# Tiles of token sums turned once per attention unit, with later loads and statistics and with stores on SyncE's queue

## The chip, the cores and the metric

One core of a Trainium2 chip runs the whole kernel. The metric is the device time of one execution in microseconds (us); smaller is better.

## The reference, cut to what matters

```python
# attention, for each of 8 batches and 8 heads, 576 tokens, head size 64
q_s = softmax(q, axis=-1)              # over the head's channels
k_s = softmax(k, axis=2)               # over the tokens
attn = q_s @ (k_s^T @ v)               # heads side by side: x [8, 576, 512]
# first mixer (weights moe_*)
h = relu(x^T @ w_tok1) @ w_tok2        # mixes tokens, 576 -> 256 -> 576
u = x + h^T
y = u + relu(u @ w_ch1) @ w_ch2        # mixes channels, 512 -> 1536 -> 512
# second mixer (weights moe2_*)
yn = (y - mean(y)) / sqrt(var(y) + 1e-6) * g_ln
out = y + relu(yn @ w2_ch1) @ w2_ch2   # 512 -> 2048 -> 512
```

## The kernel before

Each product is made of three passes on parts of float32 (PASSES), so the kernel is bound to many matmuls on TensorE (PE). The 4608 tokens are cut into nine blocks of 512: block j below 8 holds the first 512 tokens of batch j, and block 8 (B in the code) holds the 64 last tokens of every batch.

**The first mixer's channel part** is the class Phase1. A block takes 12 steps f. A step makes one tile of hidden rows (L1, line 748, PSUM tile ph), its ReLU and rest on ScalarE (ACT, line 170) and VectorE (DVE, line 171), and adds a hidden tile made two steps earlier to four accumulators (L2, line 765, tile acc). ph has two buffers, so that L1 of step f needs DVE's h of step f - 2. The order of the blocks is: two steps of block 0, block 1, the rest of block 0, blocks 2 to 7, block 8. The hidden weights of block 0 and 1 come in from HBM in the same stretch.

**Work beside the matmuls** is put into the program by a counter of ticks. `later(n, fn)` runs fn at the n-th next tick, and every step has four ticks: one within L1, one behind the ReLU, one within L2, one at the end. A tick is a place in program order, not a time: each engine goes through its own instructions in order and waits for what it needs. SyncE (SP) holds only DMA issues, so it runs ahead until one of them has to wait; what stands behind that one waits too. The same holds for DMAs that are issued on ACT, where arithmetic stands behind them.

**Attention** is the class Unit: one unit is a batch and two heads. The first eight run before the steps. Then four units run beside each block from the end of block 1 until the end of block 6, ten ticks apart (GAP), in a chain k_max (DVE, line 472), k_top (PE transpose, line 493, DVE, line 495: tile kmd), k_sub (PE transpose of kmd, line 506, tile pb; POOL, line 514, and then the loads of the next unit's k and q, on SP), q_exp, q_norm, q_split, kv (PE, line 555, and then the load of the next unit's v, on SP), tok1, hidden, tok2. q_turn turns the unit's softmax in 32x32 pieces on DVE, q_move stores that tile (zq) to HBM from ACT's queue, and q_load brings it back by rows from SP's queue, which completes the transposition for q_T.

**The sums y** of a block are completed by Phase1.finish, which runs in the second step of the next block: DVE adds u to the accumulators (line 787, tile yT, one buffer), POOL adds the rest of u for each of four chunks of 128 tokens (line 793), and yT goes to HBM as it is. For the second mixer the sums are needed by tokens too. For each chunk c, YAT + YGAP * c ticks behind finish, y_turn turns the pieces on DVE (line 678, tile z), one tick later y_move stores z from ACT's queue (line 685), three ticks after that y_load loads it by rows on SP's queue (line 692, tile yn), and three ticks after that y_stat takes mean and variance on DVE (lines 696 and 697). z and yn take turns in the two buffers of one tag. Block 8 has another way, y_store: four transposes on PE into PSUM (line 702), one copy on ACT (line 707), a store from ACT's queue (line 711), and y_stat directly on that copy.

**Root** makes 1/sqrt of the variances of blocks 0 to 6 (`Root(0, B - 1)`, 37 ticks into block 7) and brings them to HBM; a second Root does this for blocks 8 and 7 in the second mixer.

**The second mixer's weights** are prepared beside blocks 2 to 8. Sums goes through jobs, two of them per step: `first`, `bits` and `add` on DVE and ACT, `out` (ACT and POOL, lines 885 and 886, tile so), `store` (line 963, on ACT's queue), `load` (line 915, on ACT's queue). Rows (in blocks 7 and 8, one run per step) loads rows on SP (line 978, tile xr), decodes them on ACT and DVE (lines 873, 877, 880), splits them (lines 885 and 886) and stores from POOL's queue. In block 8, the second mixer's first inputs are loaded (load_x, line 1126; load_mr, line 1143), normalized by POOL (hat, line 1150), scaled by ACT (gain) and split and subtracted (lines 1159, 1160 on DVE, 1165 on POOL).

**The second mixer** follows with products (line 1263) and their sums (line 1301), with 48 steps and no attention.

Of the kernel before, what the change touches and what calls it, by code (L numbers as in the profile page):

```python
# [8 lines left out]
F32 = mybir.dt.float32  # L9
# [7 lines left out]
P = 128  # L17
# [7 lines left out]
def kernel(  # L25
# [23 lines left out]
    nc = tc.nc  # L49
    B, H, S, D = q.shape  # L50
    DM = H * D
# [18 lines left out]
    NB = NT // BLK  # L70
    CT = BLK // P
    LAG = 2
    YAT, YGAP = 3, 5
    HT = 3 * P
    SB = 2 * HT
    NS = NT // SB
# [6 lines left out]
    main = ctx.enter_context(tc.tile_pool(name="main", bufs=1))  # L83
# [7 lines left out]
    y_dram = dram.tile([NB, CT, 4, P, P], F32, name="y_dram")  # L91
    q_dram = dram.tile([2, P, W], F32, name="q_dram")
    yT_dram = dram.tile([NB, P, KD, BLK], F32, name="yT_dram")
# [81 lines left out]
    extra, bufs = [], []  # L175
# [164 lines left out]
    def later(n, fn):  # L340
        ticks.setdefault(now[0] + n, []).append(fn)
# [92 lines left out]
    class Unit:  # L434
# [7 lines left out]
        def start(self, at):  # L442
            steps = (
                self.k_max, self.k_top, self.q_max, self.q_sub, self.k_sub, self.q_exp,
                self.q_norm, self.k_exp, self.q_split, self.kv, self.tok1,
                lambda: self.q_T(0), self.hidden, lambda: self.q_T(1),
                lambda: self.tok2(0), lambda: self.tok2(1), self.q_turn, self.q_move, self.q_load,
            )
            if self.early:
                when = (0, 1, 1, 1, 3, 3, 4, 5, 7, 8, 10, 10, 11, 12, 14, 15)  # L450
            else:
                when = (0, 2, 1, 2, 4, 4, 5, 6, 8, 8, 10, 13, 12, 99, 15, 16, 7, 8, 10)
            if 0 < self.n < 3:
                k = (12, 8)[self.n - 1]
                when, steps = when[k:], steps[k:]
            for n, fn in zip(when, steps):
                if n < 99:
                    later(at + n, fn)
# [163 lines left out]
            )  # L622

        def q_move(self):
            nc.scalar.dma_start(out=q_dram[self.n % 2], in_=self.zq)

        def q_load(self):
            self.qz = self.zq
# [45 lines left out]
    yT_t, yn_t, yz = {}, {}, {}  # L674
# [7 lines left out]
        yz[j, c] = z  # L682

    def y_move(j, c):
        nc.scalar.dma_start(out=y_dram[j, c].rearrange("q t w -> (q t w)").rearrange("(p n) -> p n", p=P), in_=yz.pop((j, c)))

    def y_rows(j, c):
        return y_dram[j, c].rearrange("q t w -> t q w")
# [1 line left out]
    def y_load(j, c):  # L690
        yn_t[j, c] = main.tile([P, DM], F32, tag="t", bufs=2, name="yn")
        nc.sync.dma_start(out=yn_t[j, c].rearrange("p (q w) -> p q w", q=4), in_=y_rows(j, c))

    def y_stat(j, c, yn):
        st = main.tile([P, 6], F32, tag="st6", bufs=2, name="st6")
        nc.vector.bn_stats(out=st, in_=yn)
        nc.vector.bn_aggr(out=mr[:, pos[j], :, c], in_=st)

    def y_store(j, c):
        pt = psum("py")  # L700
        for kk in range(KD):
            nc.tensor.transpose(
                out=pt[:, kk * P:(kk + 1) * P], in_=yT_t[j][:, kk, c * P:(c + 1) * P],
                identity=ident,
            )
        yn = yn_t[j][:, c * DM:(c + 1) * DM]
        nc.scalar.activation(
            out=yn.rearrange("p (q k e) -> p k q e", q=4, k=KD), in_=pt[:, 0:DM].rearrange("p (k q e) -> p k q e", q=4, k=KD),
            func=AF.Copy,
        )  # L710
        nc.scalar.dma_start(out=y_rows(j, c), in_=yn.rearrange("p (q w) -> p q w", q=4))
        y_stat(j, c, yn)
# [7 lines left out]
    class Phase1:  # L720
# [51 lines left out]
        def finish(self, dds=range(KD)):  # L772
            if self.f1 < NF1:
                t = [main.tile([P, 512], F32, tag="t", bufs=2, name="part") for _ in range(2)]
                x = att.tile([P, 2, 512], F32, tag="qx", name="part")
                for dd, o in enumerate((t[0], t[1], x[:, 0], x[:, 1])):
                    nc.scalar.activation(out=o, in_=self.acc[dd], func=AF.Copy)
                for dd in range(2):
                    nc.sync.dma_start(out=part_dram[:, dd], in_=t[dd])
                nc.sync.dma_start(out=part_dram[:, 2:4], in_=x)  # L780
                return
            if not dds[0]:
                yT_t[self.j] = main.tile([P, KD, BLK], F32, tag="y", bufs=1, name="yT")
            yT, u = yT_t[self.j], u_t[self.j]
            for dd in dds:
                x = self.part[dd // 2][:, dd % 2] if self.f0 else u[:, 0, dd].bitcast(F32)
                nc.vector.tensor_tensor(out=yT[:, dd], in0=self.acc[dd], in1=x, op=ALU.add)
            if dds[-1] < KD - 1:
                return

            def add(c):
                x = slice(c * P, (c + 1) * P)
                nc.gpsimd.tensor_tensor(
                    out=yT[:, :, x], in0=yT[:, :, x], in1=u[:, 1, :, x].bitcast(F32), op=ALU.add
                )

            if self.j == B:
                return add
            later(26, lambda: nc.sync.dma_start(out=yT_dram[self.j], in_=yT))
            for c in range(CT):  # L800
                if self.f0 == 0:
                    later(2 * c if self.j > 1 else 0, lambda c=c: add(c))
                n = YAT + YGAP * c
                later(n, lambda c=c: y_turn(self.j, c))
                later(n + 1, lambda c=c: y_move(self.j, c))
                later(n + 4, lambda c=c: y_load(self.j, c))
                later(n + 7, lambda c=c: y_stat(self.j, c, yn_t.pop((self.j, c))))


    class Root:  # L810
# [81 lines left out]
    class Sums:  # L892


        def __init__(self):
            self.st = None
            self.jobs = [lambda: self.load(0), nop]
            for n in range(2 * NP):
                self.jobs += [
                    self.first, self.bits, self.add, lambda n=n: self.out(n, 0), self.store,  # L900
                    lambda n=n: self.out(n, 1),
                    lambda n=n: (self.store(), self.load(n + 1)), nop,
                ]

        def run(self):
# [54 lines left out]
                self.done = (wd_dram[g, :, kk], o[:, :, 0:3])  # L960

        def store(self):
            nc.scalar.dma_start(out=self.done[0], in_=self.done[1].bitcast(F32))

    class Rows:

# [37 lines left out]
    with tc.manual_schedule():  # L1004
# [162 lines left out]
        for o, f in steps:  # L1167
# [6 lines left out]
            if f == 0:  # L1174
                if 1 < o.j < B - 1:
                    for hp in range(NHP):
                        Unit((o.j + 1) * NHP + hp).start(OFF + hp * GAP)
                elif o.j == B - 1:
                    att.release()
                    w2pool = tc.alloc_tile_pool(name="w2pool", bufs=1, reuse_waits="tile")  # L1180
                    mix_rows.append(Rows(w2pool))
                    later(20, load_ends)
                    Root(0, B - 1).start(37)
            if o.j <= 1:
                loads.until(len(tok) + 4 * (f // 2) + 2)
            if o.j == B:
# [195 lines left out]
            at((0, 0, 0, 1, 3)[n - 3], (4, 5, 6, 0, 1)[n - 3], lambda n=n: load_w2(n))  # L1382
        at(1, 3, more_acc)
        at(2, 6, other_h)
        root = Root(B - 1, NB)
        at(5, 0, root.root)
        at(5, 2, root.rstd)
        at(5, 4, root.scatter)
# [88 lines left out]
```

## Time and profile before

| what | value |
|---|---|
| median of 3 runs | 1611.84 us (1611.59 to 1618.25) |
| profiled execution, its own time | 1613.86 us |
| its span, first to last instruction | 1612.1 us |
| PE busy | 1563.9 us (97%) |
| DVE, ACT, POOL busy | 892.8 us (55%), 482.8 us (30%), 511.8 us (32%) |
| mean granted clock of PE | 0.993 |
| one half step of blocks 7 and 8, 12 matmuls | 2.72 us |
| steps of blocks 2 to 6 with attention, read from block to block | 92 to 93 us for 12 steps |

Busy time of PE is near the whole span, so what counts is where PE stands still, what it waits for there, and how fast it runs (the granted clock, 1.00 for 2.4 GHz and 0.50 for 1.2 GHz). The busy times of the other engines say little, since most of their idle time is waiting for PE.

### The profile page before, as it was taken

The numbers are of one execution on the slowest core, as the hardware profiler recorded it, in microseconds if no ns is written. First come the engines' busy times: TensorE is split into PE (matmuls) and PEld (weight loads), VectorE is DVE, ScalarE is ACT, GpSimd is POOL, SyncE is SP. The second block draws the span as 40 slices with busy tenths as digits, with TensorE's granted clock in tenths as the row PEclk, the third lists the DMA queues.
The fourth block names the chain that finished last, engine by engine and source line by source line (L and its number), as shares of the span: only waits on it lengthen the run. The fifth ranks groups of instructions, "written<-read, shape, count | busy, mean of one in ns | idle before, by whom it ended". The sixth has DMA issues, their size and how long they took to land.

```text
span 1612.1 us, 21480 instructions
## 1 busy us (share of the span) xinstructions
PE 1563.9 (97%) x7993; PEld 1369.3 (85%) x7993; DVE 892.8 (55%) x1625; ACT 482.8 (30%) x976; POOL 511.8 (32%) x424
## 2 busy tenths in 40 slices
PE   5999999999999999999989999999999999999998
PEld 4988888888887878887868989999898999989897
DVE  7775657677675857757774445335335335325333
ACT  5664323333233333323231222222222222213111
POOL 5744613343342535333561402210310310311000
PEclk9999999999999999999989999999999999999999
DMA  7562534545463654548777566346355445444351
GB/s 184 162 206 72 134 122 130 165 138 172 120 179 115 175 144 137 157 155 316 231 271 274 192 144 217 130 148 206 121 174 181 148 157 176 152 150 162 115 168 39
DMA packets 212221, 263.46 MB, mean 163 GB/s; under 512 B 98958, under 2 KB 168646, under 8 KB 203670
## 3 DMA queue, kind: packets, MB, share of 16 engines
q1 hardware_dynamic: 184534, 204.22, 40.9%
q10 hardware_dynamic: 22528, 40.80, 7.7%
q0 software_dynamic: 5056, 17.08, 2.9%
q8 instruction: 63, 1.03, 0.3%
q14 instruction: 40, 0.33, 0.1%
HBM read 199.62 MB, written 62.43 MB: 163 GB/s over the span
## 4 chain that ended last, share of the span: by engine, by line
PE 82%; DMA 7%; DVE 4%; POOL 2%; ACT 2%; issue 2%; SPq 0%; ACTq 0%; DVEq 0%; POOLq 0%
PE pp L1263 22%; PE acc L1301 17%; PE ph L748 14%; PE acc L765 12%; PE acca L1301 8%; PE pu L649 4%; DMA yn<-y_dram 3%; PE pg L585 2%; PE pk L555 1%; DMA wc_dram<-so 1%; PE ph L634 1%; DMA st<-in_moe_w_ch 1%; DMA zq<-q_dram 1%; DMA stages<-in_moe_w_tok 1%; DMA y_dram<-z 1%
## 5 line engine op out<-in xcount | busy, mean ns | idle before, releaser
L1263 PE MATMUL pp<-xc,wr 128*128 128x384 f32 x2016 | 393.3, 338 | 0.0
L1263 PEld LDWEIGHTS pp<-xc,wr 128*128 128x128 f32 x2016 | 359.6, 188 | 19.3 <-DVE sc L1276 0.4
L748 PE MATMUL ph<-u,w 128*128 128x512 f32 x1296 | 325.7, 398 | 9.8 <-DVE h L171 9.8
L765 PE MATMUL acc<-h,w 128*128 128x512 f32 x1296 | 319.7, 393 | 0.0
L748 PEld LDWEIGHTS ph<-u,w 128*128 128x128 f32 x1296 | 241.1, 191 | 60.3 <-DVE h L171 11.5
L765 PEld LDWEIGHTS acc<-h,w 128*128 128x128 f32 x1296 | 238.6, 188 | 47.5
L1301 PE MATMUL acc<-w,hh 128*128 128x512 f32 x648 | 180.6, 393 | 0.0
L1301 PEld LDWEIGHTS acc<-w,hh 128*128 128x128 f32 x648 | 121.3, 188 | 26.6
L1301 PE MATMUL acc<-w,h 128*128 128x512 f32 x501 | 143.6, 394 | 0.0
L1150 POOL TENSOR_TENSOR xs<-xs 128x768 f32<-128x768 f32 x48 | 89.8, 1901 | 153.1 <-DMA xs<-mr_dram 127.9
L170 ACT ACTIVATE hh<-sc 128x384 fp32r<-128x384 f32 x96 | 50.5, 526 | 238.7 <-DVE sc L1276 236.2
L171 DVE SCALAR_TENSOR_TENSOR h<-ph,h 128x512 fp32r<-128x512 f32 x108 | 73.7, 684 | 82.3 <-ACT h L170 81.9
L1276 DVE TENSOR_TENSOR sc<-su,pp 128x384 f32<-128x384 f32 x144 | 79.6, 553 | 66.2 <-PE pp L1263 65.6
L1276 DVE TENSOR_TENSOR su<-su,pp 128x384 f32<-128x384 f32 x96 | 53.1, 553 | 111.6 <-PE pp L1263 111.2
L1301 PE MATMUL acca<-w,hh 128*128 128x512 f32 x432 | 114.2, 391 | 0.0
L170 ACT ACTIVATE h<-ph 128x512 fp32r<-128x512 f32 x108 | 64.1, 595 | 139.1 <-PE ph L748 130.6
L1301 PEld LDWEIGHTS acc<-w,h 128*128 128x128 f32 x501 | 92.5, 188 | 12.2
L171 DVE SCALAR_TENSOR_TENSOR hh<-sc,hh 128x384 fp32r<-128x384 f32 x96 | 63.6, 662 | 63.3 <-ACT hh L170 63.3
L1301 PEld LDWEIGHTS acca<-w,hh 128*128 128x128 f32 x432 | 80.5, 188 | 14.0
L886 POOL TENSOR_TENSOR so<-st,so 128x512 fp32r<-128x512 f32 (+2 forms) x48 | 40.2, 853 | 116.9 <-ACT so L885 102.3
L1321 POOL DMA_DIRECT2D out<-sd x5 | 2.9, 582 | 224.8 <-DVE sd L1314 224.8
L649 PE MATMUL pu<-w,hs 128*128 128x288 f32 x384 | 62.2, 298 | 0.0
(191 smaller groups left out, 1951.8 us busy)
## 6 DMA issues: line engine op xcount, KB each, us to landing
wr<-wc_dram SPq DMA_DIRECT2D x48, 1024.0 KB, 4.8
wr<-wd_dram SPq DMA_DIRECT2D x48, 768.0 KB, 4.4
yT_dram<-yT SPq DMA_DIRECT2D x9, 1024.0 KB, 9.1
yb<-y_dram SPq DMA_DIRECT2D x36, 256.0 KB, 6.2
y_dram<-z ACTq DMA_DIRECT2D x32, 256.0 KB, 2.6
yn<-y_dram SPq DMA_DIRECT2D x32, 256.0 KB, 3.6
st<-in_moe_w_ch ACTq DMA_DIRECT2D x16, 512.0 KB, 5.5
wc_dram<-so ACTq DMA_DIRECT2D x16, 512.0 KB, 3.1
```

Of the source, the lines that this page charges most:

```text
L170: nc.scalar.activation(out=hi, in_=x, func=AF.Relu)
L171: nc.vector.scalar_tensor_tensor(out=lo, in0=x, scalar=0.0, in1=hi.bitcast(F32), op0=ALU.max, op1=ALU.subtract)
L555: nc.tensor.matmul(out=pk[:, 0:2 * D + 2], lhsT=self.kt[:, c], rhs=vts[self.n % 2 if self.early else 0][:, c, :], start=(c == 0), stop=(c ...
L585: nc.tensor.matmul(out=pg[:, 0:T], lhsT=self.qn[:, x, c], rhs=w1[:, y, c, :], start=(n == 0), stop=(n == len(terms) - 1),)
L649: nc.tensor.matmul(out=pu[:, 0:HN], lhsT=l, rhs=r, start=(n == 0), stop=(n == len(terms) - 1))
L748: nc.tensor.matmul(out=ps, lhsT=w[:, x, kk, fo:fo + P], rhs=u[:, y, kk], start=(n == 0), stop=(n == 3 * KD - 1),)
L765: nc.tensor.matmul(out=self.acc[dd], lhsT=w[:, x, f % 2, dd * P:(dd + 1) * P], rhs=h[:, y], start=(f == self.f0 and n == 0), stop=(f == se ...
L886: nc.gpsimd.tensor_tensor(out=o[:, 1], in0=x, in1=o[:, 0].bitcast(F32), op=ALU.subtract)
L1150: nc.gpsimd.tensor_tensor(out=y, in0=y, in1=m, op=(ALU.subtract, ALU.mult)[op])
L1263: nc.tensor.matmul(out=bank[(BANK[i] + q) % 2][:, 0:HT], lhsT=r[:, kk, x], rhs=xc[i][:, y, kk], start=(n == 0 and not add), stop=(n == 5), ...
L1276: nc.vector.tensor_tensor(out=o, in0=x, in1=y, op=ALU.add)
L1301: nc.tensor.matmul(out=acc[c], lhsT=h[:, x, m * P:(m + 1) * P], rhs=wb2[p][:, f, y], start=(p == 0 and n == 0), stop=(p == NP - 1 and n == 5),
```

## The change

- YAT goes from 3 to 5 and YGAP from 5 to 10: the four chunks of a block are turned ten ticks apart, the distance of the attention units. y_load comes 5 ticks behind y_turn instead of 4, and y_stat 14 ticks behind it instead of 7.
- y_move, q_move and the stores of Sums are issued on SP's queue instead of ACT's. q_turn and q_move stand ahead of q_split and kv among the instructions of their ticks. A store of Sums is issued at once behind its `out`; the number of jobs stays eight.
- POOL's additions for blocks 2 to 6 come 3, 5, 7 and 8 ticks behind finish instead of 0, 2, 4 and 6. yT goes to HBM 18 ticks behind finish instead of 26.
- Block 7 (B - 1) uses y_store, 5, 7, 9 and 11 ticks behind finish, in place of y_turn, y_move, y_load and y_stat.
- Root for blocks 0 to 5 starts 24 ticks into block 7; the second Root takes blocks 6, 8 and 7.

```diff
-    YAT, YGAP = 3, 5
+    YAT, YGAP = 5, 10
...
-                self.q_norm, self.k_exp, self.q_split, self.kv, self.tok1,
+                self.q_norm, self.k_exp, *(() if self.early else (self.q_turn, self.q_move)), self.q_split, self.kv, self.tok1,
                 lambda: self.q_T(0), self.hidden, lambda: self.q_T(1),
-                lambda: self.tok2(0), lambda: self.tok2(1), self.q_turn, self.q_move, self.q_load,
+                lambda: self.tok2(0), lambda: self.tok2(1), self.q_load,
...
-                when = (0, 2, 1, 2, 4, 4, 5, 6, 8, 8, 10, 13, 12, 99, 15, 16, 7, 8, 10)
+                when = (0, 2, 1, 2, 4, 4, 5, 6, 7, 8, 8, 8, 10, 13, 12, 99, 15, 16, 10)
...
-            nc.scalar.dma_start(out=q_dram[self.n % 2], in_=self.zq)
+            nc.sync.dma_start(out=q_dram[self.n % 2], in_=self.zq)
...
-        nc.scalar.dma_start(out=y_dram[j, c].rearrange("q t w -> (q t w)").rearrange("(p n) -> p n", p=P), in_=yz.pop((j, c)))
+        nc.sync.dma_start(out=y_dram[j, c].rearrange("q t w -> (q t w)").rearrange("(p n) -> p n", p=P), in_=yz.pop((j, c)))
...
-        yn = yn_t[j][:, c * DM:(c + 1) * DM]
+        yn = yn_t[B][:, c * DM:(c + 1) * DM] if j == B else main.tile([P, DM], F32, tag="t", bufs=2, name="yn")
...
-            later(26, lambda: nc.sync.dma_start(out=yT_dram[self.j], in_=yT))
+            later(18, lambda: nc.sync.dma_start(out=yT_dram[self.j], in_=yT))
...
-                    later(2 * c if self.j > 1 else 0, lambda c=c: add(c))
+                    later((3, 5, 7, 8)[c] if 1 < self.j < B - 1 else 2 * c * (self.j > 1), lambda c=c: add(c))
+                if self.j == B - 1:
+                    later(5 + 2 * c, lambda c=c: y_store(self.j, c))
+                    continue
...
-                later(n + 4, lambda c=c: y_load(self.j, c))
-                later(n + 7, lambda c=c: y_stat(self.j, c, yn_t.pop((self.j, c))))
+                later(n + 5, lambda c=c: y_load(self.j, c))
+                later(n + 14, lambda c=c: y_stat(self.j, c, yn_t.pop((self.j, c))))
...
-                    self.first, self.bits, self.add, lambda n=n: self.out(n, 0), self.store,
-                    lambda n=n: self.out(n, 1),
-                    lambda n=n: (self.store(), self.load(n + 1)), nop,
+                    self.first, self.bits, self.add, lambda n=n: (self.out(n, 0), self.store()), nop,
+                    lambda n=n: (self.out(n, 1), self.store()),
+                    lambda n=n: self.load(n + 1), nop,
...
-            nc.scalar.dma_start(out=self.done[0], in_=self.done[1].bitcast(F32))
+            nc.sync.dma_start(out=self.done[0], in_=self.done[1].bitcast(F32))
...
-                    Root(0, B - 1).start(37)
+                    Root(0, B - 2).start(24)
...
-        root = Root(B - 1, NB)
+        root = Root(B - 2, NB)
```

## Rows read from the trace of the kernel before

**Rows 1.** Windows by stretch: us, busy (x instructions) by engine, clock, DMA share, GB/s

```profile
85.00:805.00 720.00, 705.92 (x3600) 596.98 (x3599) 485.21 (x898) 250.36 (x511) 290.72 (x254) 1.00 0.53 159
805.00:860.00 55.00, 47.22 (x199) 39.10 (x198) 37.89 (x38) 15.93 (x28) 26.99 (x19) 0.91 0.64 240
860.00:1612.00 752.00, 745.91 (x3715) 671.14 (x3713) 307.06 (x512) 165.38 (x316) 137.67 (x99) 1.00 0.49 161
```

**Rows 2.** Waits of PE from 85 to 805 us: total us, times, longest

```profile
PE pb L506 <- DVE kmd L495: 8.5, 9, 2.3
PE ph L748 <- DVE h L171: 2.0, 2, 1.3
```

**Rows 3.** Timeline from 427 to 581 us: start, duration, operation [idle before <- releaser]

```profile
428.09 0.32 PE L506 MATMUL pb<-ident,kmd 128*128 128x128 f32 x1 [0.19 <-DVE kmd L495]
...
570.37 1.31 SPq L692 DMA_DIRECT2D yn<-y_dram  x1
...
578.53 0.69 DVE L696 BATCH_NORM_STATS2 st<-yn 128x6 f32<-128x512 f32 x1 [6.42 <-DMA yn<-y_dram]
...
580.75 0.32 PE L506 MATMUL pb<-ident,kmd 128*128 128x128 f32 x1 [2.33 <-DVE kmd L495]
```

**Rows 4.** Waits of DVE from 85 to 705 us

```profile
DVE st L696 <- DMA yn<-y_dram: 28.2, 5, 6.4
```

**Rows 5.** Windows of the three stretches at the lower clock behind 85 us

```profile
581.29:584.70 3.41, 3.41 (x13) 2.92 (x12) 2.86 (x3) 0.72 (x2) 1.71 (x1) 0.50 0.03 8
809.98:816.80 6.82, 5.08 (x12) 4.02 (x13) 6.72 (x9) 2.16 (x4) 3.72 (x3) 0.50 0.42 151
833.88:837.28 3.40, 3.40 (x9) 2.64 (x8) 2.17 (x2) 0.00 (x0) 2.44 (x2) 0.50 1.02 425
```

**Rows 6.** Waits of PE from 805 to 860 us

```profile
PE ph L748 <- DVE h L171: 7.7, 2, 5.1
```

**Rows 7.** Timelines of DVE and POOL from 800 to 834 us

```profile
802.51 0.69 DVE L696 BATCH_NORM_STATS2 st<-yn 128x6 f32<-128x512 f32 x1 [6.84 <-DMA yn<-y_dram]
...
805.67 4.43 DVE L880 SCALAR_TENSOR_TENSOR xr<-xr 128x512 uint32<-128x512 uint32 x1
810.03 1.07 DVE L678 STREAM_TRANSPOSE z<-yT 128x512 f32<-128x512 f32 x1
...
825.24 7.43 DVE L1160 TENSOR_TENSOR xc<-xs,xc 128x768 fp32r<-128x768 f32 x1
...
805.98 3.57 POOL L1150 TENSOR_TENSOR xs<-xs 128x768 f32<-128x768 f32 x2
...
822.82 7.25 POOL L1150 TENSOR_TENSOR xs<-xs 128x768 f32<-128x768 f32 x4
```

**Rows 8.** DMA issues of the page: count, KB each, median us from issue to landing

```profile
y_dram<-z ACTq DMA_DIRECT2D x32, 256.0 KB, 2.6
yn<-y_dram SPq DMA_DIRECT2D x32, 256.0 KB, 3.6
...
y_dram<-xs ACTq DMA_DIRECT2D x4, 256.0 KB, 8.0
```

**Rows 9.** Lines of PE, then its timeline around the first such group

```profile
L702 PE MATMUL py<-ident,yT 128*128 128x128 f32 x16 | 2.4, 272 | 0.0
...
861.58 0.60 PE L702 MATMUL py<-ident,yT 128*128 128x128 f32 x4
...
861.93 1.29 PE L1263 MATMUL pp<-xc,wr 128*128 128x384 f32 x6
```

**Rows 10.** Waits of SP from 85 to 705 us, then timelines of SP and DVE

```profile
SPq L353 <- POOL kt L514: 139.8, 23, 10.1
...
449.45 1.25 SPq L353 DMA_DIRECT2D rawk<-in_k  x2
...
460.19 1.28 DVE L472 TENSOR_REDUCE kmx<-rawk 128x128 f32<-128x640 f32 x1
```

**Rows 11.** POOL's additions to yT by duration: ns least, median, most

```profile
L793 POOL TENSOR_TENSOR yT<-yT,u x32: 1272/1299/1886, 173.0 to 862.6; 128x512 f32<-128x512 f32 x32
```

## The prediction

> **What bounds the kernel now.** I read the totals first, then windows by stretch, then PE's waits, and then the timeline at each wait. PE is busy for 97% of the span, so no engine that becomes lighter helps by itself; what can be won is where PE stands or runs slowly. Windows behind the start-up show where [rows 1]: PE stands for 720.0 - 705.9 = 14.1 us from 85 to 805 us, for 7.8 us in the short stretch from 805 to 860, and for 6.1 us in the 752 us behind that, which are the end of the program. The second mixer is therefore not touched by anything here. In the middle stretch the clock is below full speed too (0.91), so its loss is larger than its idle time.
>
> PE's waits name the reason. Between 85 and 805 us PE waits nine times for kmd, 8.5 us in all, and twice for h, 2.0 us [rows 2]. The timeline shows how the largest wait comes about [rows 3]: SP issues the load of yn at 570.37, DVE reaches the statistics and stands for 6.42 us until the load lands, and only at 578.53 does it go on; kmd stands behind the statistics, and PE stands for 2.33 us. DVE has five such waits for yn before block 7, 28.2 us in all [rows 4], one in each of five blocks; PE has five waits for kmd of 1.1 to 2.3 us at the same places. The other four are like the 0.19 us at 428 [rows 3] and belong to the chain of the unit itself. So the late part is 8.5 - 4 x 0.2 = 7.7 us.
>
> The windows at half clock [rows 5] each lie behind a wait of PE: 3.41 us behind the 2.33 us at 580.75, 6.82 us beginning within the 5.1 us wait and 3.40 us behind the 2.6 us wait of the stretch from 805 on [rows 6]. At half clock half of the time is lost: 1.7 us for the first, 5.1 us for the two others.
>
> In that stretch PE waits for h of DVE, 5.1 and 2.6 us [rows 6]. DVE's and POOL's timelines tell why [rows 7]. DVE stands 6.84 us for yn of block 7. That moves the decoding of xr behind 803 us, where POOL begins to normalize the next input. L880 takes 4.43 us while two POOL operations of 3.57 us run; the turn of z (1.07 us) stands behind it, and then h. Later L1160 takes 7.43 us beside four POOL operations of 7.25 us, and h stands behind that one.
>
> **The change, part by part.**
>
> *Statistics later (blocks 0 to 6).* y_stat stands 13 ticks behind y_move instead of 6, and 9 behind y_load instead of 3. A tick is 92.5/48 = 1.9 us in blocks 2 to 6 and 2.72/2 = 1.4 us in block 7. Store and load take 2.6 + 3.6 us by median [rows 8]; the load that came late took 578.5 - 570.4 = 8.1 us. Nine ticks are 17 us, in block 7 12 us, so the load would have to take over twice as long as the late one. I take DVE's five waits as gone, and the 7.7 us of PE with them, and the 1.7 us of slow clock. The two waits for h in block 7, 2.0 us, stand behind the same statistics of block 6; they go too. What is late next on DVE is k_max, which needs the load of k (below). Sum: -11.4 us.
>
> *Stores on SP.* ACT loses these issues, 32 of them for z alone [rows 8], and the waits in front of them. PE's waits [rows 2] name ACT in none, so nothing is won by this alone; I count nothing. SP gains the same issues, each of which can hold up what stands behind. Between two units SP has the loads of k and q, of v, of q by rows and of y by rows; now also q_move, y_move and about one store of Sums. The loads of k already wait for POOL 139.8 us in 23 times [rows 10], so SP is ahead of its producers, and new waits first use that up. A late load of k would show on DVE: in the unit shown, the load begins at 449.45 and k_max at 460.19 [rows 10]; two issues take 1.25 us, the third half of that, and with the 3.6 us of yn [rows 8] for its landing there are about 5 us of slack. A store of Sums waits for one POOL operation of some 1.3 us and ACT ahead of it. Lower bound 0, upper bound: see the rival. I take 0.
>
> The Trainium skill says (DMA: Bandwidth & Descriptors, section "Issuing engines are not separate DMA queues") that DMAs of all issuing engines run on the same 16 DMA engines, and that using several issuers saves only the time of the issuing. By it the move makes no transfer faster or slower; the sum above counts none.
>
> *Additions on POOL later.* The last addition comes at tick 15 of the block, one tick before the next unit writes the same buffer u. One addition takes 1.3 us [rows 11]. If it is late, ACT waits for it: at most 5 x 1.3 = 6.5 us of ACT, of which PE sees what exceeds the two-step slack of h. Nothing below: it removes no wait of PE. I take 1 us for it and all other new waits in blocks 2 to 6.
>
> *Block 7 on TensorE.* Added: 16 transposes on PE, 4 copies on ACT, 4 stores. The same line in the second mixer takes 0.60 us for four as drawn, but the next matmul begins 861.93 - 861.58 = 0.35 us behind the first [rows 9], so 4 x 0.35 = 1.4 us; the upper bound is 16 x 0.272 = 4.4 us. I take 1.5 us, because PE's pipeline was full there as it will be here. Removed: four turns of 1.07 us on DVE, four loads, and DVE's wait of 6.84 us. The statistics now need ACT's copy, and the third and fourth copy need a buffer that a store must have left. The stores of that way took 8.0 us [rows 8]; issued some 5 us before the third copy would start, they can hold ACT for about 3 us, ahead of the h which has over 4 us left. So I expect the decoding (L873 to L880) to be done at about the time when POOL begins, and h no longer to stand behind it.
>
> The Trainium skill (TensorE: Matmul & The Clock Gate, section "Part 4: PE-mode transpose") gives about 275 ns for a transpose in a kernel's context. The row's 272 ns as drawn agrees; by it the sum would be 4.4 us for the sixteen, while the row of starts gives 1.4 us.
>
> *The stretch from 805 on.* It loses 7.7 us in waits and 5.1 us in slow clock, 12.8 us. The first wait with its clock is 5.1 + 3.4 = 8.5 us, and I take it as gone. Of the second, 2.6 + 1.7 = 4.3 us, I take half: its POOL operations come earlier since SP no longer stands in front of the load of means (two loads of yn hold SP there), but PE comes earlier as well. Sum: -10.7 us; bounds -12.8 and 0.
>
> *Root.* It does the same work in two parts; the second mixer has no idle time to lose or win. 0.
>
> Sum: -7.7 - 1.7 - 2.0 - 10.7 + 1.5 + 1.0 = -19.6 us. Against the profiled execution, 1613.86 us, that is 1594.3; that execution was 2.0 us above the median, so I forecast 1611.84 - 19.6 = 1592 us.
>
> **The rivals.**
>
> *POOL still lies on DVE at the transition.* The waits for kmd and h in blocks 2 to 7 go, but block 8 keeps its first wait, because the copy or the statistics of the fourth chunk come too late and the decoding again meets POOL's normalization. For it: the margin is about 1 us by my count, and L880 and L1160 show that any such operation of DVE is held as long as POOL's run of operations. Against it: z and the wait for yn are gone. Price: 8.5 us come back, 1600.7; if both waits stay, 10.7, 1603.
>
> The Trainium skill (SBUF — State Buffer, section "Who interferes with whom") speaks for this one: an operation of DVE with two inputs in SBUF and one of GpSimd which reads SBUF exclude each other for the whole instruction, and the order of issue decides. Both rows agree with it, 4.43 us beside 3.57 and 7.43 beside 7.25. By it removing z alone would win 1.07 us of the first wait.
>
> *Nothing measurable.* The waits for kmd are replaced by others of the chain, for example DVE waiting for the turned q or k, so that only part of the 11.4 us and little at the transition is won: 1604 to 1612. Against it: the four small waits show that without a late yn the chain costs 0.2 us.
>
> *Slower: SP's queue becomes the bound.* A store of z or so that waits on DVE or POOL stops the loads of k, q and v behind it. It decides once a load of k comes over 5 us later than now: k_max then waits on DVE, kmd and PE with it, in up to 24 units. At 1.5 us a unit, 36 - 19.6 gives 1628; the break-even is 0.8 us a unit. For it: y_move, which used to stop ACT, now stops the queue that feeds attention. Against: each store's producer stands earlier in program order than the load behind it.
>
> **How the numbers follow.** About 0.5% (8 us) is what a measurement of this kernel can tell from no change. The forecast, 1587 to 1598, gets 0.60; the rival at the transition, 1598 to 1605, 0.20; nothing measurable 0.12; slower 0.08. Faster than 1603.8 is the first and nearly all of the second, 0.80; within 0.5% 0.13; slower 0.07. The range, 1586 to 1605, reaches from the full gain (all of the 12.8 us, -21.7, with some us for waits that I don't see) to the second case's upper end.
>
> **What would show it.** Right: no wait of DVE for yn in blocks 2 to 7; PE's waits for kmd only of about 0.2 us; no slow window near 580; sixteen more L702 in block 8 with 0.35 us per four; L880 behind the load of means no longer at 4 us. Wrong: DVE waiting for rawk or rawq, PE waiting for pk or kmd in units that did not wait before, ACT waiting for POOL's additions, or two waits for h with slow clock behind 800 us as before.

## The result and the profile after

The changed kernel takes 1587.56 us (median of 4, 1586.72 to 1587.93) against 1612.46 us of the kernel before on the same chip: ratio 0.9837, 95% interval 0.9814 to 0.9861, so some 25 us faster. The forecast was 1592 us with a range from 1586 to 1605; it held, near its fast end. The profiled execution took 1587.23 us, its span is 1585.4 us, 26.7 us less than before.

Windows of the changed kernel by stretch (the transition lies about 22 us earlier than in [rows 1], so the stretches are cut at 783 and 836):

```profile
85.00:783.00 698.00, 694.44 (x3576) 590.20 (x3575) 482.51 (x899) 249.83 (x511) 288.73 (x252) 1.00 0.53 162
783.00:836.00 53.00, 52.96 (x246) 44.82 (x245) 31.73 (x32) 18.82 (x32) 32.84 (x21) 1.00 0.70 274
836.00:1586.00 750.00, 743.21 (x3700) 668.80 (x3698) 303.45 (x509) 163.96 (x314) 135.04 (x98) 1.00 0.49 159
```

PE stands for 3.6 and 0.0 us in the first two stretches, where it stood for 14.1 and 7.8 us [rows 1]: 18.3 us less. The clock is at full speed in all three, so the half-clock windows [rows 5] are gone. PE was busy in them for 3.41 + 5.08 + 3.40 us, and half of that is 5.9 us. The transposes add 1.4 us (below). That is -18.3 - 5.9 + 1.4 = -22.8 us.

Where the 26.7 us lie is seen from two marks, PE's first matmul of the steps and the first product of the second mixer, first in the kernel before, then in the changed one:

```profile
85.45 8.39 PE L748 MATMUL ph<-u,w 128*128 128x512 f32 x36
...
843.25 1.21 PE L1263 MATMUL pp<-xc,wr 128*128 128x384 f32 x6
```
```profile
83.95 8.38 PE L748 MATMUL ph<-u,w 128*128 128x512 f32 x36
...
816.54 1.21 PE L1266 MATMUL pp<-xc,wr 128*128 128x384 f32 x6
```

From mark to mark it is 757.8 us before and 732.6 after: the first mixer's steps take 25.2 us less, of which 2.4 us are put down to nothing here. The rest of the program takes 768.8 us in both. The other 1.5 us lie ahead of the first mark. They do not belong to the change: in a second profile of the changed kernel (experiment 10) that mark stands at 85.59 us.

Waits of PE from 85 to 836 us (total us, times, longest), to be held against [rows 2, 6]:

```profile
PE pu L649 <- ACT qT L163: 1.3, 2, 0.8
PE pu L649 <- DVE qT L165: 0.9, 2, 0.5
PE pb L506 <- DVE kmd L495: 0.7, 4, 0.2
PE pk L555 <- ACT kt L527: 0.6, 1, 0.6
```

The four waits for kmd of 0.2 us that belong to the unit's own chain are left, the five long ones are gone, and h is in the list no more. DVE, which stood 28.2 us for yn [rows 4], now has this one row at the statistics from 85 to 836 us, and it is block 7's wait for ACT's copy:

```profile
DVE st L696 <- ACT yn L707: 1.9, 1, 1.9
```

Timeline of the changed kernel around the transition, the counterpart of [rows 7] and [rows 9]. Its lines from 805 on stand three further than before, so L880 and L883 here are lines 877 and 880 there:

```profile
769.52 0.60 PE L702 MATMUL py<-ident,yT 128*128 128x128 f32 x4
769.87 0.48 PE L748 MATMUL ph<-u,w 128*128 128x512 f32 x1
...
781.17 0.69 DVE L696 BATCH_NORM_STATS2 st<-yn 128x6 f32<-128x512 f32 x1 [1.92 <-ACT yn L707]
...
783.20 0.69 DVE L883 SCALAR_TENSOR_TENSOR xr<-xr 128x512 uint32<-128x512 uint32 x1
...
784.50 1.83 POOL L1153 TENSOR_TENSOR xs<-xs 128x768 f32<-128x768 f32 x1 [7.10 <-DMA xs<-mr_dram]
...
788.49 3.65 POOL L1153 TENSOR_TENSOR xs<-xs 128x768 f32<-128x768 f32 x2
792.09 1.31 POOL L889 TENSOR_TENSOR xr<-xr 128x512 fp32r<-128x512 f32 x1
...
788.25 5.71 DVE L880 SCALAR_TENSOR_TENSOR xr<-xr 128x512 uint32<-128x512 uint32 x1
793.99 2.72 DVE L883 SCALAR_TENSOR_TENSOR xr<-xr 128x512 uint32<-128x512 uint32 x1
796.63 0.68 DVE L171 SCALAR_TENSOR_TENSOR h<-ph,h 128x512 fp32r<-128x512 f32 x1
...
797.36 2.60 PEld L748 LDWEIGHTS ph<-u,w 128*128 128x128 f32 x12 [0.36 <-DVE h L171]
```

The first decoding ends at 783.9 us, 0.6 us before POOL begins to normalize. The next step's decoding still falls upon POOL: L880 takes 5.71 us, L883 2.72. But no z and no wait for yn stands ahead of them, and DVE begins h at 796.63. PE's weight load waits 0.36 us for it and its matmuls do not pause, where they waited 5.1 and 2.6 us [rows 6]. The Trainium skill (SBUF — State Buffer, section "Who interferes with whom") says that an operation of DVE with two inputs in SBUF and one of GpSimd that reads SBUF exclude each other, and that the order of issue decides. The length agrees: L880 ends at 793.96, behind three operations of POOL that run from 788.49 to 793.40, and POOL's own take no longer than elsewhere. The order cannot be read from these rows, since L880 is drawn as beginning 0.24 us ahead of POOL's first and is yet the one that is held. Four transposes still cost PE 769.87 - 769.52 = 0.35 us.

### The profile page after: what moved, and what is told of

The parts are those of the page before. It is cut to its first block, busy times and chain, and to the rows that moved or that the text cites. A ratio compares the mean times of both kernels' runs of the same rounds, so it can differ in the third digit from the quotient of the medians.

```text
span 1585.4 us, 21496 instructions
## 1 busy us (share of the span) xinstructions
PE 1555.8 (98%) x8009; PEld 1365.6 (86%) x8009; DVE 882.0 (56%) x1621; ACT 484.2 (31%) x980; POOL 513.0 (32%) x424
## 4 chain that ended last, share of the span: by engine, by line
PE 92%; DVE 3%; DMA 2%; ACT 1%; POOL 1%; issue 1%; SPq 0%; DVEq 0%; POOLq 0%; ACTq 0%
PE pp L1266 22%; PE ph L748 17%; PE acc L765 17%; PE acc L1304 17%; PE acca L1304 8%; PE pu L649 4%; PE pg L585 3%; PE pk L555 2%; PE ph L634 1%; DMA zq<-q_dram 1%; DMA stages<-in_moe_w_tok 1%; DMA q_dram<-zq 0%; DVE km L486 0%; DVE st L935 0%; DVE kmx L472 0%
## 5 line engine op out<-in xcount | busy, mean ns | idle before, releaser
L748 PE MATMUL ph<-u,w 128*128 128x512 f32 x1296 | 320.7, 394 | 0.0
L748 PEld LDWEIGHTS ph<-u,w 128*128 128x128 f32 x1296 | 237.8, 188 | 48.3 <-DVE h L171 0.4
L171 DVE SCALAR_TENSOR_TENSOR hh<-sc,hh 128x384 fp32r<-128x384 f32 x96 | 60.7, 633 | 63.3 <-ACT hh L170 63.3
L499 POOL TENSOR_TENSOR qt<-rawq,qm 128x640 f32<-128x640 f32 x24 | 31.8, 1325 | 109.0 <-DVE qm L478 106.3
```

The lines of the kernel that those rows point to most:

```text
L171: nc.vector.scalar_tensor_tensor(out=lo, in0=x, scalar=0.0, in1=hi.bitcast(F32), op0=ALU.max, op1=ALU.subtract)
L499: nc.gpsimd.tensor_tensor(out=self.qt, in0=self.qr.rearrange("p h c d -> p c h d"), in1=self.qm.unsqueeze(3).to_broadcast([P, NC + 1, 2, D ...
L748: nc.tensor.matmul(out=ps, lhsT=w[:, x, kk, fo:fo + P], rhs=u[:, y, kk], start=(n == 0), stop=(n == 3 * KD - 1),)
```

## The experiments

In each, the time is a median, the ratio is to the kernel before on the same chip, with its 95% interval. "After" means the edit was made to the changed kernel, "before" to the other one.

**1. The three stores on ACT again (after).**

```diff
-  nc.sync.dma_start(out=q_dram[self.n % 2], in_=self.zq)
+  nc.scalar.dma_start(out=q_dram[self.n % 2], in_=self.zq)
...
-  nc.sync.dma_start(out=self.done[0], in_=self.done[1].bitcast(F32))
+  nc.scalar.dma_start(out=self.done[0], in_=self.done[1].bitcast(F32))
...
-  self.first, self.bits, self.add, lambda n=n: (self.out(n, 0), self.store()), nop,
-  lambda n=n: (self.out(n, 1), self.store()),
-  lambda n=n: self.load(n + 1), nop,
+  self.first, self.bits, self.add, lambda n=n: self.out(n, 0), self.store,
+  lambda n=n: self.out(n, 1),
+  lambda n=n: (self.store(), self.load(n + 1)), nop,
```

y_move is changed in the same way, and q_turn and q_move go back to their old place.

> The changed kernel with the three stores (z, zq, so) on ACT's queue again, with the old order of the jobs and of q_move. If the gain comes from the later statistics and from block 7 on TensorE, and the queue counts for nothing, this stays within 4 us of the changed kernel's 1588 us, with PE's waits for kmd still at about 0.2 us each. If the gain comes from ACT being rid of the stores and their waits, 10 us or more come back, to 1598 us or above, and waits of PE for h or kmd return.

Measured: 1593.81 us, 0.9865 (0.9845 to 0.9884), 5.8 us above the changed kernel's second measurement (experiment 10), between the two forecasts. The two intervals overlap a little, but the fastest of these runs, 1592.56 us, is slower than the slowest of those, 1589.1. The trace says where it goes. Waits of PE, then a timeline of ACT:

```profile
PE ph L634 <- ACT gs L590: 6.1, 4, 1.5
```
```profile
346.17 0.39 ACTq L966 DMA_DIRECT2D wc_dram<-so  x1
349.26 0.64 ACT L888 ACTIVATE so<-st 128x256 fp32r<-128x256 f32 x2 [3.22 <-DMA wc_dram<-so]
...
349.80 0.37 ACT L590 ACTIVATE gs<-pg 128x256 f32<-128x256 f32 x1
```

ACT may write so again only when the store of its first half has landed. Issued one job later, on ACT, that store holds ACT for 3.22 us; the copy gs stands behind, and PE waits for it in four units, 6.1 us. Issued at once from SP, the store has landed in time: ACT's waits for it fall from 40.3 us in eleven to 1.4 us in one, and the changed kernel has no such row of PE. Issued at once from ACT, it was not tried. The kernel before had the row too, smaller because PE itself came later (in the unit near 350 us, gs begins at 350.08 us before and at 350.03 in experiment 4, and PE waits 0.50 and 1.27 us for it):

```profile
PE ph L634 <- ACT gs L590: 2.0, 4, 0.5
```

**2. Loads and statistics early again, spacing kept (after).**

```diff
-  later(n + 5, lambda c=c: y_load(self.j, c))
-  later(n + 14, lambda c=c: y_stat(self.j, c, yn_t.pop((self.j, c))))
+  later(n + 4, lambda c=c: y_load(self.j, c))
+  later(n + 7, lambda c=c: y_stat(self.j, c, yn_t.pop((self.j, c))))
```

> The changed kernel with the load of yn 4 ticks and the statistics 7 ticks behind the turn again, at the new distance of ten ticks. If lateness is what matters, DVE waits for yn again and PE for kmd behind it: 4 to 9 us more than the changed kernel, 1592 to 1597 us. If it is the even spacing, one chunk per attention unit, that matters, DVE's waits stay away and the time stays at 1587 to 1589 us.

Measured: 1589.93 us, 0.9842 (0.9818 to 0.9865). DVE waits for yn only six times, 8.5 us in all, the longest 2.7; no long wait for kmd comes back. What comes is a wait of PE for kmx, 2.7 us in four units. With the chunks ten ticks apart and the stores on SP, the late statistics are worth 2 us at most, which the intervals do not tell from nothing. So in this company it is not the lateness that removes the waits for kmd, as the second forecast had it.

**3. Block 7 turned on DVE again (after).**

```diff
-  later(5 + 2 * c, lambda c=c: y_store(self.j, c))
+  n = 3 + 5 * c
+  later(n, lambda c=c: y_turn(self.j, c))
+  later(n + 1, lambda c=c: y_move(self.j, c))
+  later(n + 4, lambda c=c: y_load(self.j, c))
+  later(n + 7, lambda c=c: y_stat(self.j, c, yn_t.pop((self.j, c))))
```

> The changed kernel with block 7's sums turned on DVE again, at the old distances, stores on SP. If the gain behind 780 us comes from block 7 on TensorE, PE's waits for h with slow clock come back in block 8: 5 to 13 us less 1.4 us of transposes, 1592 to 1600 us. If it comes from the other parts (SP's queue, earlier loads), the time stays at 1586 to 1588 us.

Measured: 1587.08 us, 0.9824 (0.9804 to 0.9845): no loss, the second forecast. PE's waits for h come to 1.7 us in two, the longest 1.3, with no half-clock window. A timeline of DVE at the transition:

```profile
783.39 0.69 DVE L696 BATCH_NORM_STATS2 st<-yn 128x6 f32<-128x512 f32 x1 [4.69 <-DMA yn<-y_dram]
...
785.00 0.69 DVE L884 SCALAR_TENSOR_TENSOR xr<-xr 128x512 uint32<-128x512 uint32 x1
785.73 2.25 DVE L887 SCALAR_TENSOR_TENSOR xr<-xr 128x512 uint32<-128x512 uint32 x1
787.90 1.11 DVE L678 STREAM_TRANSPOSE z<-yT 128x512 f32<-128x512 f32 x1
788.92 0.65 DVE L171 SCALAR_TENSOR_TENSOR h<-ph,h 128x512 fp32r<-128x512 f32 x1
```

Lines 884 and 887 here are 877 and 880 of the kernel before. The wait for yn and the turn of z stand ahead of h as there [rows 7], but the wait is 4.69 us instead of 6.84 and the decoding is held for 2.25 us, not 4.43. Beside the other edits, block 7 on TensorE is worth nothing that shows.

**4. Only the late statistics of blocks 0 to 6, and Root in two other parts (before).**

```diff
+  late = self.j < B - 1
-  n = YAT + YGAP * c
+  n = 5 + 10 * c if late else YAT + YGAP * c
...
-  later(n + 4, lambda c=c: y_load(self.j, c))
-  later(n + 7, lambda c=c: y_stat(self.j, c, yn_t.pop((self.j, c))))
+  later(n + (5 if late else 4), lambda c=c: y_load(self.j, c))
+  later(n + (14 if late else 7), lambda c=c: y_stat(self.j, c, yn_t.pop((self.j, c))))
```

> The kernel before with only the new spacing and the later loads and statistics for blocks 0 to 6, and Root split to allow it; stores on ACT, block 7 as before. If the statistics are the cause in blocks 2 to 7, 11 us of the gain are here: 1601 us, with PE's waits for kmd at 0.2 us each and block 8's two waits for h unchanged. If the stores on SP are needed for it, 1606 to 1613 us.

Measured: 1599.53 us, 0.9898 (0.988 to 0.9917), 16.5 us faster. Waits of PE from 85 to 860 us:

```profile
PE ph L634 <- ACT gs L590: 5.2, 4, 1.3
PE ph L748 <- DVE h L171: 4.9, 2, 4.6
PE pb L506 <- DVE kmd L495: 0.8, 4, 0.2
```

The waits for kmd are gone, as forecast, by this edit alone. It holds three things, the spacing, the later load and the later statistics, and which of them does it is not separated here. The transition was forecast to keep both waits and keeps one long one, 4.6 us, with 6.8 us at half clock; so the gain is larger than forecast. The wait for gs grows from 2.0 to 5.2 us, since PE now comes earlier to the same late copy.

**5. Only block 7 on TensorE (before).**

```diff
+  if self.j == B - 1:
+      later(5 + 2 * c, lambda c=c: y_store(self.j, c))
+      continue
```

y_store's tile is changed as in the diff.

> The kernel before with only block 7's sums turned by TensorE (stores on ACT, old distances, early statistics for blocks 0 to 6). If turning on DVE is what holds h in block 8, the two waits of PE for h and their slow clock (12.8 us) go, 1.4 us of transposes are added: about 1601 us, and the five waits for kmd stay. If POOL's holding of DVE is the cause whichever engine turns, only the 1 us of the turn is won: 1610 to 1613 us.

Measured: 1607.79 us, 0.9957 (0.9942 to 0.9972), 6.9 us faster, between the two forecasts. PE's waits for h fall from 9.8 us in four (85 to 860 us) to 0.3 in one, and no half clock is left at the transition. But those for kmd are 11.5 us where the kernel before had 8.5, with three half-clock windows of 3.4 us in place of one. The edit changes nothing in blocks 2 to 6, where these waits lie, so this rise is a difference between executions and hides a part of the gain.

**6. The stores of Sums one job later, still on SP (after).** The jobs as in the new lines of experiment 1, nothing else. The expectation speaks of the first half's store; the second half's comes a job later too.

> The changed kernel with the old order of jobs in Sums, so that the first half of so is stored one job later, still on SP's queue. With stores on ACT, PE waited four times 1.5 us for gs, since ACT stood for so's first half to land in front of the copy of gs. If the late store is what makes that wait, it comes back here: 4 to 6 us more than the changed kernel. If the store's place on ACT's queue makes it, the time stays within 1.5 us of the changed kernel.

Measured: 1642.32 us, 1.0168 (1.015 to 1.0186), 54 us above the changed kernel and far outside both forecasts. A timeline of SP, ACT, POOL and PE around the first long wait, then PE's waits, then the window of one of six stretches at half clock:

```profile
279.30 1.33 POOL L889 TENSOR_TENSOR so<-st,so 128x512 fp32r<-128x512 f32 x1 [6.75 <-issue]
...
283.19 1.57 POOL L514 TENSOR_TENSOR kt<-rawk,kb 128x640 f32<-128x640 f32 x1 [1.35 <-ACT kb L510]
...
284.79 1.22 SPq L353 DMA_DIRECT2D rawk<-in_k  x2
...
288.04 0.59 SPq L799 DMA_DIRECT2D yT_dram<-yT  x1
288.73 0.38 SPq L966 DMA_DIRECT2D wc_dram<-so  x1
...
294.73 0.63 ACT L888 ACTIVATE so<-st 128x256 fp32r<-128x256 f32 x2 [9.28 <-DMA wc_dram<-so]
...
295.61 0.74 ACT L527 ACTIVATE kt<-kt 128x640 f32<-128x640 f32 x1
...
296.40 1.02 PE L555 MATMUL pk<-vt,kt 128*128 128x130 f32 x3 [6.09 <-ACT kt L527]
```
```profile
PE pk L555 <- ACT kt L527: 30.2, 5, 6.4
PE ph L634 <- ACT gs L590: 10.7, 4, 3.1
```
```profile
295.53:302.35 6.82, 5.95 (x19) 5.18 (x20) 5.22 (x12) 2.24 (x6) 2.66 (x4) 0.50 0.40 99
```

POOL has so ready at 280.6. The store of it comes in SP's order behind the load of k, which waits for POOL's k_sub (line 514), and behind the 1 MB of yT; it is issued at 288.73, and ACT stands 9.28 us until it has landed. kt stands behind that on ACT, and PE waits 6.09 us for kt. So the two edits of the diff, SP's queue and the store at once, belong together: the changed kernel with the first and without the second is slower than the kernel before.

**7 and 8. The store of zq on ACT in its old place; POOL's additions at the old ticks (each alone, after).**

```diff
-  nc.sync.dma_start(out=q_dram[self.n % 2], in_=self.zq)
+  nc.scalar.dma_start(out=q_dram[self.n % 2], in_=self.zq)
```
```diff
-  later((3, 5, 7, 8)[c] if 1 < self.j < B - 1 else 2 * c * (self.j > 1), lambda c=c: add(c))
+  later(2 * c * (self.j > 1), lambda c=c: add(c))
```

> The changed kernel with zq's store and turn in their old order on ACT's queue; z and so on SP. PE's remaining waits of 0.5 to 0.9 us are for qT, which comes from zq. If SP's queue delays zq, they go, 0 to 2 us are won: 1586 to 1588 us. If ACT in front of the store is slower, waits for qT or kvs grow: 1589 us or more.

> The changed kernel with POOL's additions to yT at their old ticks (0, 2, 4, 6). ACT waited 15 us in five times for the last addition in the changed kernel. If PE's slack covers it, as I hold now, the time stays within 1 us of 1588 us, with ACT's wait gone. If my 1 us for it was real, 1586 to 1587 us.

Measured: 1588.19 us, 0.9818 (0.9804 to 0.9833), and 1589.31 us, 0.9827 (0.9811 to 0.9844). Neither can be told from the changed kernel. With the later additions ACT does wait for them, 15.2 us in five waits (4.1 in one with the old ticks), but PE's waits are as short in both. So the store of zq on SP and the later additions are worth nothing that shows beside the other edits. The earlier store of yT (18 ticks instead of 26) was not tried by itself.

**9. Only the three stores on SP, with the store at once and zq's turn earlier (before).** The reverse of experiment 1, on the other kernel.

> The kernel before with only the stores of z, zq and so on SP's queue, with the new order of jobs and of q_move; old distances, early statistics, block 7 on DVE. After the first four experiments I hold that the queue removes waits too: z is stored as soon as DVE has turned it, so yn comes earlier; then DVE's wait for yn falls under half of 43 us and the time to 1595 to 1603 us. If only the lateness of the statistics matters, DVE's waits and the five waits for kmd stay, and the time is 1607 to 1613 us.

Measured: 1595.64 us, 0.9881 (0.9866 to 0.9896), 19.2 us faster, the largest gain of the three parts alone. Waits of PE (85 to 860 us), waits of DVE (85 to 705 us), and the place of [rows 3] in the timeline:

```profile
PE ph L748 <- DVE h L171: 3.9, 1, 3.9
PE pu L649 <- DVE qT L165: 2.8, 5, 1.1
PE pb L506 <- DVE kmd L495: 1.5, 7, 0.3
...
DVE st L696 <- DMA yn<-y_dram: 21.3, 5, 4.4
```
```profile
572.49 0.69 DVE L696 BATCH_NORM_STATS2 st<-yn 128x6 f32<-128x512 f32 x1 [4.38 <-DMA yn<-y_dram]
...
574.71 0.32 PE L506 MATMUL pb<-ident,kmd 128*128 128x128 f32 x1 [0.28 <-DVE kmd L495]
```

The time came out as forecast, and the reason given for it did not: DVE's wait for yn was to fall under half of 43 us and is 35.0 of 43.2 us from 85 to 860 us. In the five blocks it is still 21.3 us, three quarters of what it was, and yet PE's waits for kmd come to 1.5 us. The wait for kmd is DVE's wait less 4.1 us: 4.38 gives 0.28 here, 6.42 gave 2.33 [rows 3]. Of 20 such pairs in the kernel before and in experiments 5, 11 and 12, all lie within 0.02 us of that, or at zero below it (3.73 gives 0). So it was enough to bring the yn wait down to about 4.1 us; it did not have to vanish.

**10. The changed kernel once more**, on the chip of experiments 5, 6 and 9.

> The changed kernel once more, on the same chip as the others, to compare them with: 1587 to 1590 us, and in its trace again no wait of PE above 1 us between 85 us and the end.

Measured: 1588.0 us (1587.54 to 1589.1), 0.9835 (0.9819 to 0.9852); the longest wait of PE from 85 us on is 0.6 us. As forecast.

**11 and 12. One store moved alone (each before): z's; the store of Sums, at once.**

In 11 y_move's `nc.scalar` becomes `nc.sync`; in 12 the store of Sums, with the new order of the jobs:

```diff
-  nc.scalar.dma_start(out=self.done[0], in_=self.done[1].bitcast(F32))
+  nc.sync.dma_start(out=self.done[0], in_=self.done[1].bitcast(F32))
```

> The kernel before with only z's store on SP's queue. In all runs so far PE's wait for kmd was DVE's wait for yn in front of it less 4.1 us. If z's own place on ACT's queue is what makes yn late, the waits for yn come under 4.5 us here, PE's waits for kmd to 0.3 us, and some 8 to 15 us are won: 1600 to 1607 us. If ACT is late for another reason (so's halves), z is late in any case and the time stays above 1609 us.

> The kernel before with only so's stores on SP's queue and issued at once (new order of jobs); z and zq on ACT. If ACT standing for so's first half (32 us) is what makes z late, the waits for yn come under 4.5 us and 8 to 15 us are won: 1600 to 1607 us. If not, only the waits of 0.5 us for gs go, 2 us: 1610 to 1614 us.

Measured: 1607.47 us, 0.9938 (0.9923 to 0.9953), and 1604.49 us, 0.9921 (0.9905 to 0.9937). They are 10.0 and 12.8 us faster, and neither for the reason looked for. With z's store on SP the yn waits stay (29.9 us in five), and so do the waits for kmd (10.2 us in nine); its trace has less waiting at the transition, where h is waited for once, 4.1 us. With the store of Sums on SP, yn is waited for 24.6 us in five and kmd 5.2 us in eight: closer, but only one of five yn waits falls below 4.1. The traces account for only part of these gains: their spans lie 6.7 and 6.0 us below that of the kernel before, whose profiled execution, 1613.86 us, was faster than all that ran beside these two experiments (1616.13 to 1619.25 us). So by PE's waits for kmd neither does what experiment 9 does (1.5 us). The store of zq was not moved alone. One row points to it. Waits of SP from 85 to 705 us, of the kernel before and of experiment 9:

```profile
SPq L629 <- DMA q_dram<-zq: 63.3, 20, 13.9
```
```profile
SPq L629 <- DMA q_dram<-zq: 8.6, 7, 3.4
```

SP, with the loads of yn behind it, waited 63.3 us for the store of zq to land when ACT issued it; 66.6 us in experiment 11, 41.2 in experiment 12, 8.6 in experiment 9. Such a wait need not cost anything: in experiment 7, with late statistics, it is 45.0 us and nothing is lost. Whether that store makes the rest of the difference alone stays open.

## Why the prediction came out right, and which step failed

The table adds up, for every kernel, PE's listed waits from 85 to 860 us and half of the time spent at half clock in that stretch. What is left of the span is nearly the same for all, 1579 to 1585 us, so these two columns are most of what the edits change. Idle time within a half-clock window counts in both columns, by some 0.9 us in the kernel before and most in experiment 6.

```
kernel                       waits  clock   span    span less both
before                       21.9   6.8   1612.1   1583.4
changed                       3.5   0.0   1585.4   1581.9
changed again (10)            2.4   0.0   1586.0   1583.6
1  stores on ACT              7.7   0.0   1592.0   1584.3
2  statistics early           4.2   0.0   1587.0   1582.8
3  block 7 on DVE             4.4   0.0   1584.9   1580.5
4  late statistics only      11.5   3.4   1598.0   1583.1
5  block 7 only              15.8   5.1   1606.1   1585.2
6  stores a job later        43.6  20.5   1642.7   1578.6
7  zq's store on ACT          3.6   0.0   1587.8   1584.2
8  additions early            2.9   0.0   1586.2   1583.3
9  queue only                 8.8   1.7   1592.9   1582.4
11 z's store only            17.3   6.8   1605.4   1581.3
12 Sums' store only          17.0   6.8   1606.1   1582.3
```

**Right.** The statistics later: -7.7 us was forecast for kmd, and 8.5 fell to 0.7; experiment 4 shows that this part does it alone. The slow window at 580 us went with it. The transposes: 1.4 us. Root: nothing shows. The account by waits and clock was the right one.

**Right in size, not shown in cause.** Three terms of the sum were put down to one edit each, and the runs do not bear that out. The waits for kmd were put down to the lateness of the statistics; with the stores on SP the spacing does without it (experiment 2), and whether the spacing would also do on ACT's queue was not tried. The 2.0 us for h in block 7 were put down to the same edit; they are gone in experiments 5, 9, 11 and 12 too, which keep the early statistics. The transition was put down to block 7 on TensorE; that edit alone does remove its waits (experiment 5), but the other edits remove all but 1.7 us of them without it (experiment 3). In each case more than one edit of the change cures the same wait. That the sum held with nothing counted for the queue is partly luck of this kind.

**The step that failed** is "PE's waits [rows 2] name ACT in none, so nothing is won by this alone; I count nothing", for the stores on SP. The list of waits did name ACT, in the row of gs (2.0 us in four) that is shown with experiment 1, and I passed over it. More than that: I took the late yn as a matter of when the statistics are asked for, and did not ask what makes the load late. The queue is one of its causes: alone it wins 19.2 us, more than any other part, and in company about 5 us, by the wait for gs that would otherwise have grown to 6.1. The Trainium skill (DMA: Bandwidth & Descriptors, section "Issuing engines are not separate DMA queues") says that another issuing engine saves only issue time. The stores of z do not become faster: by median they land 3.2 to 3.3 us behind their issue from SP (the changed kernel, experiments 7, 9 and 11) and 2.1 to 2.6 us from ACT (the kernel before, experiments 1 and 12); why is open. What the queue changed is what stands in front of a store and who waits for it, and the nothing that I counted beside that rule was 19.2 us (experiment 9).

**Mis-sized terms.** I gave the transition 10.7 of 12.8 us; nearly all of its loss went. The 12.8 us were themselves some 0.9 us too many: of the 6.82 us at half clock PE was busy for 5.08 [rows 5], and the rest counts among the 5.1 us of waiting already. I gave 1.0 us for new waits; the rows of PE that are new, for ACT's qT and kt, come to 1.9 us in the first profile of the changed kernel and to 0.6 us in the second. Experiment 8 shows that the additions cost PE nothing, although ACT's waits for them, 15.2 us, exceed the bound of 6.5 us that I set. So the forecast was low in gain by some 2 us at the transition and 2 us for the wait for gs, about the 4.4 us between 1592 and 1587.56.

**The parts overlap.** Alone they win 16.5, 19.2 and 6.9 us (experiments 4, 9, 5), 42.6 in sum; together 26.6 (experiment 10). Late statistics and the queue both take the waits for kmd away; each of the three takes part of the transition. The 6.9 us carry the difference between executions named there. So a sum over edits is right only if each wait is counted once, as the forecast did.

**The rivals.** POOL does still lie on DVE, as the first said (line 880 of the kernel before takes 2.72 us in place of 4.43, but the line ahead of it 5.71), but h delays the weight load by 0.36 us and no matmul, so that it costs nothing. That nothing measurable would be left is refuted by the ratio. The slower one, SP's queue as the bound, did not come, but one edit away from the change it does: experiment 6. Its route was another than I drew: not the load of k comes late, but a store waits behind that load, and ACT behind the store.

## What to carry to other kernels

When a DMA is moved to another queue, ask for each store who waits for it to land (a buffer's next writer) and what will stand in front of it in the new queue; the move of three stores was worth -19 us alone, and the changed kernel with the stores of Sums a job later stood 27 us above the kernel before. When an engine waits off the critical path, measure the slack between its wait and PE's (4.1 us here): it is enough to push the wait below it. Edits that cure the same wait do not add up, so take each out of the changed kernel before keeping all: block 7 on TensorE could go without loss.

## What the runs showed of the hardware

The half clock does not follow from the length of PE's wait alone. Timeline of experiment 11 at two waits for kmd, and the windows behind them:

```profile
301.82 0.32 PE L506 MATMUL pb<-ident,kmd 128*128 128x128 f32 x1 [1.96 <-DVE kmd L495]
...
584.17 0.32 PE L506 MATMUL pb<-ident,kmd 128*128 128x128 f32 x1 [2.27 <-DVE kmd L495]
```
```profile
302.83:306.24 3.41, 3.41 (x14) 3.12 (x13) 2.41 (x3) 0.28 (x2) 1.43 (x1) 0.50 0.19 43
584.20:594.20 10.00, 10.00 (x57) 8.85 (x58) 9.35 (x20) 4.32 (x9) 4.46 (x4) 1.00 0.25 61
```

The wait of 1.96 us was followed by 3.41 us at half clock, the longer one of 2.27 us by none. In the kernel before, one of 2.33 us was followed by such a window [rows 5], one of 1.83 us not. Between runs the two lie further apart: a wait of 1.85 us in experiment 5 (until 679.72 us) was followed by 3.41 us at half clock, one of 2.86 us in experiment 6 (until 566.39 us) by none. At each of the five waits of some 6 us in experiment 6 the clock was at half for 6.8 us. A window that belongs to a long wait can begin before the wait ends: there at 295.53 us, 0.87 us before PE goes on at 296.40.
